# A GpSimd drain placed in the last expert of a fused linear-attention and mixture-of-experts kernel

## The chip, the core and the metric

The kernel runs on one core of a Trainium2 chip. The metric is the device time of one execution in microseconds (us); a version's time is the median of its runs. Engine names in the profile: PE is TensorE (PEld its weight loads), DVE is VectorE, ACT is ScalarE, POOL is GpSimd, SP is SyncE. A name with a q behind it (POOLq, SPq) is that engine's sequencer: semaphore waits, branches, register loads and drains run there and are not counted as busy.

## The reference

A decayed linear attention (4 batches, 8 heads, 768 steps, head dimension 64) makes 3072 token rows of 512 values, and a noisy top-2 gate sends each row to two of eight experts:

```python
state = gamma[None, :, None, None] * state + np.einsum('bhd,bhe->bhde', k[:, :, t], v[:, :, t])
y[:, :, t] = scale * np.einsum('bhd,bhde->bhe', q[:, :, t], state)
...
noisy_logits = logits + noise_scale * noise
top2 = np.argpartition(-noisy_logits, 2, axis=1)[:, :2]
...
h = np.maximum(x[mask] @ w1[e], 0.0)
out[mask] += top2_w[mask, k, None] * (h @ w2[e])
```

w1 is 512x1024 and w2 1024x512 for each expert.

## The kernel before

**The first part** (to about 100 us) does the attention in 24 chunks of 128 tokens and writes the normalized rows to `xbuf` in HBM. GpSimd has elementwise work here: `v_scale` (L302) and `q_scale` (L308), 46 instructions in all.

**The second part** handles the experts one after the other; the seven after the first are taken in an order that the counts decide. Each expert has room for 768 to 832 rows, held as blocks of 128. Row numbers per block lie in `idx`. For every block `gather` (L728) fetches rows of `xbuf` by an indirect DMA that GpSimd issues, and a DMA transpose that SP issues (L735) turns them into `xe`.

**The first layer**, `mm1` (L860 to L862), multiplies in fp16 pieces: four k-tiles of three products each (high by high, high by low, low by high), 12 matmuls per 128 hidden units, over up to half of the expert's columns. ScalarE writes the relu `hh` (L863) and VectorE the remainder `hl` (L864). There are eight such groups (`f`) in a set, and mostly two sets (`cols`) per expert. The counter `n` numbers the groups through all sets of an expert: 0 to 7 in the first, 8 to 15 in the second.

**The second layer**, `mm2` (L892 to L894), makes 24 matmuls per block of 128 rows; ScalarE scales the result into the tile `ot` (L876, four buffers), and `put` (L881) adds it to the rows of `out` by an indirect DMA with an add, again issued by GpSimd. A put waits for its `ot` from ScalarE and, since all puts add into the same tensor, for the landing of the put before it.

**Order.** The program is written under a manual schedule: each engine's queue holds its instructions in the order in which the Python code issues them. In the last expert (`e == E - 1`, room 768, six blocks) there is no next expert to gather for, so GpSimd's queue holds six puts and nothing else. With `ready = 3` the puts of blocks 0 to 2 are issued between the two sets of `mm1`, those of blocks 3 to 5 after the second set:

```python
for n0, n1 in cols:
    if n0 and ready:
        for t in range(ready):
            put(e, t, mm2(e, t))
    for f in range(FT):
        mm1(e, n0, n1, f)
```

**The end.** Behind the last put every engine reads the number of left-over blocks (L1078) and branches over the loop at L1080, which would handle rows beyond the experts' room; none are left here, so the body is not run. Then each engine waits for the outstanding DMAs and engines (semaphore waits at L1080). Leaving the tile context (L1175) ends the program: each engine runs a drain, the engines meet at a barrier led by GpSimd, GpSimd clears the semaphores, and a second barrier follows. L1171 stands for what runs ahead of the program: a drain on each engine and a few memsets on GpSimd.

Of the kernel before, what the change touches and what calls it, by code (L numbers as in the profile page):

```python
# [26 lines left out]
E, F = 8, 1024  # L27
# [70 lines left out]
def moe_kernel(ctx, tc, qT, kT, kt, vt, noise, wgn, w1, w2, ctab, qtab, xbuf, out):  # L98
    nc = tc.nc
# [83 lines left out]
    def w_load(e, which, i, n=1):  # L183

        if i == 0:
            ST[which, e] = (wpool.tile([128, 4096], F32, name="wst" + which),
                            work.tile([128, 4], F32, name="wss" + which),
                            work.tile([128, 2], F32, name="wsc" + which, bufs=3))
        src = w1 if which == "1" else w2
        src = src[ds(order[e - 1], 1)].rearrange("a p c -> (a p) c") if e else src[0]  # L190
        nc.sync.dma_start(ST[which, e][0][:, i * 1024:(i + n) * 1024], src[:, i * 1024:(i + n) * 1024])

    def w_sum(e, which, i):
        st, ss, sc = ST[which, e]
        nc.scalar.activation(junk, st[:, i * 1024:(i + 1) * 1024], AF.Square, accum_out=ss[:, i:i + 1])  # L195
        if i == 3 and e != 1:
            w_cast(e, which)

    def w_cast(e, which):
        WB[which, e] = work.tile([128, 4], BF, name="wsb" + which)  # L200
        nc.vector.tensor_copy(WB[which, e], ST[which, e][1])

    def w_scale(e, which):
        st, ss, sc = ST[which, e]
        nc.tensor.matmul(SUM[:, :4], oneb, WB[which, e], start=True, stop=True, skip_group_check=True)
        s1 = work.tile([128, 1], F32, name="s1")
        nc.vector.tensor_reduce(s1, SUM[:, :4], axis=AX.X, op=OP.add)
        pow2(s1, TW1 if which == "1" else TW2, sc[:, 0:1], sc[:, 1:2])
# [6 lines left out]
    def w_hi(e, which, i):  # L215
        st, ss, sc = ST[which, e]
        hi, lo = w_parts(which, i)
        nc.scalar.activation(hi, st[:, i * 1024:(i + 1) * 1024], AF.Copy, scale=sc[:, 0:1])  # L218

    def w_lo(e, which, i):  # L220
        st, ss, sc = ST[which, e]
        hi, lo = w_parts(which, i)
        nc.vector.scalar_tensor_tensor(lo, st[:, i * 1024:(i + 1) * 1024], sc[:, 0:1], hi,  # L223
                                       op0=OP.mult, op1=OP.subtract)
# [491 lines left out]
    def block(e, t):  # L716

        return t * 128, min(128, CAPS[e] - t * 128), NBLK * e + t

    def blocks(e):  # L720
        return range(-(-CAPS[e] // 128))

    def gather(e, t):
        o, n, i = block(e, t)
        if t == 0:
            XE[e] = XP[e % 2].tile([128, 2 * KT, CAP], F16, name="xe")
        x = XP[0].tile([128, 2 * DM], F16, name="xg", bufs=4)
        nc.gpsimd.indirect_dma_start(  # L728
            out=x[:n], out_offset=None, in_=xbuf[:128 + B0 * S] if e == 0 and t < 3 else xbuf,
            in_offset=bass.IndirectOffsetOnAxis(ap=idx[:n, i:i + 1], axis=0))  # L730
        XG[e, t] = x

    def x_t(e, t):
        o, n, i = block(e, t)
        nc.sync.dma_start_transpose(XE[e][:, :, o:o + n], XG.pop((e, t))[:n])  # L735
# [115 lines left out]
    def mm1(e, n0, n1, f):  # L851
        MM[0] += 1
        third = MM[1] and MM[0] % 3 == 0
        p = (psum2[0] if third else psum).tile([128, 512], F32, name="pH", **(dict(tag="pX") if third else dict(tag="pA", bufs=2)))
        n = n1 - n0
        for k in range(KT):
            whi = WT["1h"][:, k, f * 128:(f + 1) * 128]
            wlo = WT["1l"][:, k, f * 128:(f + 1) * 128]
            xh, xl = XE[e][:, k, n0:n1], XE[e][:, KT + k, n0:n1]
            nc.tensor.matmul(p[:, :n], whi, xh, start=(k == 0), stop=False)  # L860
            nc.tensor.matmul(p[:, :n], whi, xl, start=False, stop=False)  # L861
            nc.tensor.matmul(p[:, :n], wlo, xh, start=False, stop=(k == KT - 1))  # L862
        nc.scalar.activation(hh[:, f, n0:n1], p[:, :n], AF.Relu)  # L863
        nc.vector.scalar_tensor_tensor(hl[:, f, n0:n1], p[:, :n], 0.0, hh[:, f, n0:n1], op0=OP.max, op1=OP.subtract)  # L864

    def out_scale(e, n0, n1):
        i2 = work.tile([128, 1], F32, name="i2")
        nc.vector.tensor_tensor(i2, ST["1", e][2][:, 1:2], ST["2", e][2][:, 1:2], op=OP.mult)
        if e not in GS:
            GS[e] = work.tile([128, NBLK], F32, name="gse")  # L870
        nc.vector.tensor_scalar(GS[e][:, n0:n1], wacc[:, NBLK * e + n0:NBLK * e + n1], i2, None, op0=OP.mult)
# [7 lines left out]
    def put(e, t, ot):  # L879
        o, n, i = block(e, t)  # L880
        nc.gpsimd.indirect_dma_start(  # L881
            out=out, out_offset=bass.IndirectOffsetOnAxis(ap=idx[:n, i:i + 1], axis=0),
            in_=ot[:n], in_offset=None, compute_op=OP.add)

    def mm2(e, t, meanwhile=None):
        o, n, i = block(e, t)
        p = psum2[0].tile([128, DM], F32, name="pO", tag="pY", bufs=2)
        for f in range(FT):
            if f == 4 and meanwhile:
                meanwhile()  # L890
            a, c = hh[:, f, o:o + 128], hl[:, f, o:o + 128]
            nc.tensor.matmul(p, a, WT["2h"][:, f, :], start=(f == 0), stop=False)  # L892
            nc.tensor.matmul(p, a, WT["2l"][:, f, :], start=False, stop=False)  # L893
            nc.tensor.matmul(p, c, WT["2h"][:, f, :], start=False, stop=(f == FT - 1))  # L894
        return scaled(e, t, p)
# [122 lines left out]
    for e in range(E):  # L1018
        half = (CAPS[e] + 31) // 32 * 16
        cols = [(FIRST, 640), (640, CAPS[0])] if e == 0 else [(0, half), (half, CAPS[e])]  # L1020
        if e == 1:
            cols = [(0, 256), (256, 512), (512, CAPS[e])]
        n, more = 0, e + 1 < E

        if more:
            ahead = [lambda t=t: (gather(e + 1, t), x_t(e + 1, t)) for t in blocks(e + 1)]
        ready = 3 if not more else 0
# [3 lines that stand above are left out]
                    put(e, t, mm2(e, t))  # L1031
            for f in range(FT):
                mm1(e, n0, n1, f)
                if e:
                    if n == 2:
                        w_scale(e, "2")
                        out_scale(e, 0, NBLK)
                    if 3 <= n < 7:
                        w_hi(e, "2", n - 3)
                    if 4 <= n < 8:  # L1040
                        w_lo(e, "2", n - 4)
                    if more and n == 2:
                        w_load(e + 1, "1", 0, 2)
                        w_load(e + 1, "1", 2, 2)
                if e == 0 and n >= 7 and n < 15:
                    w_sum(1, "12"[(n - 7) // 4], (n - 7) % 4)
                if more and e and len(cols) * FT - 5 <= n < len(cols) * FT - 1:
                    w_sum(e + 1, "1", n - (len(cols) * FT - 5))
                if e == 0 and n == 14:
                    w_cast(1, "1")  # L1050
                if e == 0 and n in (1, 4, 7, 10, 13):
                    rest(1)
                n += 1
        if more and e:
            w_load(e + 1, "2", 0, 2)
            w_load(e + 1, "2", 2, 2)
            w_scale(e + 1, "1")
        todo = list(range(3, NBLK)) if e == 0 else list(blocks(e))[ready:]
        for n, t in enumerate(todo):
            if more and ahead and (e or n):  # L1060
                ahead.pop(0)()
            put(e, t, mm2_tail(e, t) if block(e, t)[1] < 128 else mm2(e, t, tables if e + n == 0 else None))
            if e == 0 and n == 0:
                w_scale(1, "1")
                w_cast(1, "2")
            if more:
                for i in ((2 * n, 2 * n + 1) if e == 0 else (n,)):
                    if i < 4:
                        w_hi(e + 1, "1", i)
                    if 1 <= i < 5:  # L1070
                        w_lo(e + 1, "1", i - 1)
                if e and 2 <= n < 6:
                    w_sum(e + 1, "2", n - 2)
            if e == 0 and n == 2:
                rank_caps()
                loop_table()
# [102 lines left out]
```

## Time and profile before

| | |
|---|---|
| median of 3 runs | 666.76 us (666.29 to 667.3) |
| the profiled execution's own time | 669.18 us |
| its span, first to last instruction | 666.9 us |
| mean granted TensorE clock | 0.99 |
| PE busy (matmuls) | 640.8 us, 96% |
| POOL busy | 201.9 us, 30%, 158 instructions |

The span is 2.28 us shorter than the profiled execution's own time, and the profiled execution is 2.42 us longer than the median of the runs. PE is at work nearly throughout; the stretch in which it is not is the end, which the 40 slices of the page show as a last digit of 1.

A row of a line's view reads: line, engine, operation and count, then shortest, median and longest duration in ns, then the starts of the first and the last one in us. A row of the timeline reads: start in us, duration in us, engine, line, operation, and in brackets how long the engine had been idle and what ended that.

### The profile page before, as it was taken

The numbers are of one execution on the slowest core, as the hardware profiler recorded it, in microseconds if no ns is written. First come the engines' busy times: TensorE is split into PE (matmuls) and PEld (weight loads), VectorE is DVE, ScalarE is ACT, GpSimd is POOL, SyncE is SP. The second block draws the span as 40 slices with busy tenths as digits, with TensorE's granted clock in tenths as the row PEclk, the third lists the DMA queues.
The fourth block names the chain that finished last, engine by engine and source line by source line (L and its number), as shares of the span: only waits on it lengthen the run. The fifth ranks groups of instructions, "written<-read, shape, count | busy, mean of one in ns | idle before, by whom it ended". The sixth has DMA issues, their size and how long they took to land.

```text
span 666.9 us, 12060 instructions
## 1 busy us (share of the span) xinstructions
PE 640.8 (96%) x4849; PEld 387.1 (58%) x4849; DVE 301.5 (45%) x723; ACT 296.3 (44%) x538; POOL 201.9 (30%) x158
## 2 busy tenths in 40 slices
PE   8999999999979999999999999999999999999991
PEld 5998887648648744554455445544554465455540
DVE  5668786799776311532153216322622262214110
ACT  5668665214525534453454344434444454433210
POOL 3555453042243034203420343034304330340111
PEclk9999999999989999999999999999999999999996
DMA  9999986967397748764675476547645782661212
GB/s 316 385 397 399 356 283 148 370 158 235 90 143 162 226 66 133 184 175 73 117 192 170 77 116 149 208 79 126 182 159 97 115 245 84 124 117 29 32 17 33
DMA packets 91001, 112.80 MB, mean 169 GB/s; under 512 B 57248, under 2 KB 57888, under 8 KB 87360
## 3 DMA queue, kind: packets, MB, share of 16 engines
q1 hardware_dynamic: 78736, 84.95, 41.5%
q0 software_dynamic: 11344, 26.22, 22.0%
q10 hardware_dynamic: 864, 0.84, 0.4%
q8 instruction: 39, 0.64, 0.4%
q14 instruction: 18, 0.15, 0.1%
HBM read 72.67 MB, written 26.21 MB: 148 GB/s over the span
## 4 chain that ended last, share of the span: by engine, by line
PE 73%; DVE 7%; DMA 3%; issue 3%; ACT 1%; POOL 1%; SPq 0%; POOLq 0%; ACTq 0%
PE pH L860 12%; PE pH L861 12%; PE pH L862 12%; PE pO L892 11%; PE pO L894 11%; PE pO L893 11%; DMA xe<-xg 2%; PE pT L906 1%; PE pT L379 1%; DVE bb L615 1%; PE pY L353 1%; DVE hl L864 1%; DMA out<-ot,idx 1%; PE pA L331 1%; DVE w2l L230 1%
## 5 line engine op out<-in xcount | busy, mean ns | idle before, releaser
L881 POOL DMA_INDIRECT out<-ot,idx x54 | 90.5, 1677 | 338.7 <-ACT ot L876 201.4
L860 PE MATMUL pH<-xe,w1h 128*128 128x384 f16 (+5 forms) x576 | 181.6, 315 | 4.3 <-DMA xe<-xg 3.6
L861 PE MATMUL pH<-xe,w1h 128*128 128x384 f16 (+5 forms) x576 | 181.6, 315 | 0.0
L862 PE MATMUL pH<-xe,w1l 128*128 128x384 f16 (+5 forms) x576 | 181.5, 315 | 0.0
L893 PE MATMUL pO<-w2l,hh 128*128 128x512 f16 x384 | 145.5, 379 | 0.4 <-DVE w2l L230 0.4
L894 PE MATMUL pO<-w2h,hl 128*128 128x512 f16 x384 | 145.5, 379 | 0.1
L892 PE MATMUL pO<-w2h,hh 128*128 128x512 f16 x384 | 145.5, 379 | 0.0
L864 DVE SCALAR_TENSOR_TENSOR hl<-pH,hh 128x384 f16<-128x384 f32 (+5 forms) x144 | 75.2, 527 | 131.1 <-ACT hh L863 129.9
L863 ACT ACTIVATE hh<-pH 128x384 f16<-128x384 f32 (+5 forms) x144 | 67.2, 468 | 135.3 <-PE pH L862 113.9
L876 ACT ACTIVATE ot<-pO,gse 128x512 f32<-128x512 f32 x48 | 33.2, 691 | 171.4 <-PE pO L894 157.6
L223 DVE SCALAR_TENSOR_TENSOR w1l<-wst,wsc,w1h 128x1024 f16<-128x1024 f32 x28 | 35.8, 1284 | 105.3 <-ACT w1h L218 105.3
L860 PEld LDWEIGHTS <-w1h 128*128 128x128 f16 x576 | 56.5, 98 | 37.0 <-issue 6.4
L728 POOL DMA_INDIRECT xg<-xbuf,idx x54 | 57.5, 1065 | 66.6 <-DVE wacc L636 31.9
L861 PEld LDWEIGHTS <-w1h 128*128 128x128 f16 x576 | 56.5, 98 | 31.5 <-issue 1.4
L862 PEld LDWEIGHTS <-w1l 128*128 128x128 f16 x576 | 56.6, 98 | 31.2
L195 ACT ACTIVATE junk<-wst 128x1024 bf16<-128x1024 f32 x64 | 67.3, 1051 | 0.0
L894 PEld LDWEIGHTS <-hl 128*128 128x128 f16 x384 | 37.6, 98 | 46.6 <-issue 1.0
L892 PEld LDWEIGHTS <-hh 128*128 128x128 f16 x384 | 37.6, 98 | 44.7 <-ACT junk L195 0.3
L893 PEld LDWEIGHTS <-hh 128*128 128x128 f16 x384 | 37.6, 98 | 44.0
L302 POOL TENSOR_TENSOR vp<-in_v,cs 128x512 f32<-128x512 f32 x24 | 26.3, 1095 | 45.6 <-issue 15.2
L218 ACT ACTIVATE w2h<-wst,wsc 128x1024 f16<-128x1024 f32 x32 | 36.6, 1142 | 1.4 <-DVE wsc L173 1.4
L218 ACT ACTIVATE w1h<-wst,wsc 128x1024 f16<-128x1024 f32 x32 | 36.2, 1141 | 1.2 <-DVE wsc L173 1.2
(168 smaller groups left out, 607.6 us busy)
## 6 DMA issues: line engine op xcount, KB each, us to landing
wst<-w SPq DMA_DIRECT2D x28, 1024.0 KB, 7.2
in_q<-qT SPq DMA_DIRECT2D x24, 256.0 KB, 5.7
in_k<-kT SPq DMA_DIRECT2D x24, 256.0 KB, 4.5
in_v<-vt SPq DMA_DIRECT2D x24, 256.0 KB, 5.5
in_kt<-kt SPq DMA_DIRECT2D x24, 256.0 KB, 6.2
xbuf<-x SPq DMA_DIRECT2D x24, 256.0 KB, 5.4
out<-zero SPq DMA_DIRECT2D x6, 1024.0 KB, 5.9
wst<-w SPq DMA_DIRECT2D x8, 512.0 KB
```

The costliest lines, as they stand in the source:

```text
L195: nc.scalar.activation(junk, st[:, i * 1024:(i + 1) * 1024], AF.Square, accum_out=ss[:, i:i + 1])
L218: nc.scalar.activation(hi, st[:, i * 1024:(i + 1) * 1024], AF.Copy, scale=sc[:, 0:1])
L728: nc.gpsimd.indirect_dma_start(out=x[:n], out_offset=None, in_=xbuf[:128 + B0 * S] if e == 0 and t < 3 else xbuf, in_offset=bass.IndirectO ...
L860: nc.tensor.matmul(p[:, :n], whi, xh, start=(k == 0), stop=False)
L861: nc.tensor.matmul(p[:, :n], whi, xl, start=False, stop=False)
L862: nc.tensor.matmul(p[:, :n], wlo, xh, start=False, stop=(k == KT - 1))
L863: nc.scalar.activation(hh[:, f, n0:n1], p[:, :n], AF.Relu)
L864: nc.vector.scalar_tensor_tensor(hl[:, f, n0:n1], p[:, :n], 0.0, hh[:, f, n0:n1], op0=OP.max, op1=OP.subtract)
L881: nc.gpsimd.indirect_dma_start(out=out, out_offset=bass.IndirectOffsetOnAxis(ap=idx[:n, i:i + 1], axis=0), in_=ot[:n], in_offset=None, com ...
L892: nc.tensor.matmul(p, a, WT["2h"][:, f, :], start=(f == 0), stop=False)
L893: nc.tensor.matmul(p, a, WT["2l"][:, f, :], start=False, stop=False)
L894: nc.tensor.matmul(p, c, WT["2h"][:, f, :], start=False, stop=(f == FT - 1))
```

## The change

Two lines are added. When the third group of the second set has been issued in the last expert (`n == 10`), a drain is issued on GpSimd's queue. It waits for no semaphore and signals none. In GpSimd's queue it stands behind the put of block 2 and ahead of the wait and the put of block 3. No other engine's instructions differ, and on GpSimd all others keep their order and their semaphores.

```diff
             for f in range(FT):
                 mm1(e, n0, n1, f)
+                if e == E - 1 and n == 10:
+                    nc.gpsimd.drain()
                 if e:
                     if n == 2:
                         w_scale(e, "2")
```

## Rows read from the trace of the kernel before

**Rows 1.** The page: the span in 40 slices (PE, POOL) and the chain that ended last.
```profile
span 666.9 us, 12060 instructions
...
PE   8999999999979999999999999999999999999991
...
POOL 3555453042243034203420343034304330340111
...
PE 73%; DVE 7%; DMA 3%; issue 3%; ACT 1%; POOL 1%; SPq 0%; POOLq 0%; ACTq 0%
```

**Rows 2.** Timeline of GpSimd in the last expert: the six puts.
```profile
612.22 1.56 POOL L881 DMA_INDIRECT out<-ot,idx  x1 [13.49 <-ACT ot L876]
619.16 1.56 POOL L881 DMA_INDIRECT out<-ot,idx  x1 [5.38 <-DMA out<-ot,idx]
624.65 1.56 POOL L881 DMA_INDIRECT out<-ot,idx  x1 [3.94 <-ACT hh L863]
643.40 1.56 POOL L881 DMA_INDIRECT out<-ot,idx  x1 [17.19 <-ACT ot L876]
648.95 1.56 POOL L881 DMA_INDIRECT out<-ot,idx  x1 [3.99 <-ACT ot L876]
654.35 1.56 POOL L881 DMA_INDIRECT out<-ot,idx  x1 [3.84 <-DMA out<-ot,idx]
```

**Rows 3.** Line 1175, the end of the program: drains and barrier waits by engine.
```profile
L1175 POOLq EVENT_SEMAPHORE  x4: 17/17/17, 666.2 to 666.8; - x4
L1175 SPq DRAIN  x3: 7/7/13, 659.9 to 666.4; - x3
L1175 POOLq DRAIN  x3: 51/103/5616, 660.5 to 666.7; - x3
L1175 ACTq DRAIN  x2: 8/8/8, 660.1 to 666.4; - x2
L1175 DVEq DRAIN  x2: 10/14/17, 660.3 to 666.4; - x2
L1175 PEldq DRAIN  x2: 8/8/8, 660.6 to 666.4; - x2
```

**Rows 4.** Line 1175 again, in the window 656 to 666.2 us alone.
```profile
L1175 POOLq DRAIN  x1: 5616/5616/5616, 660.5 to 660.5; - x1
```

**Rows 5.** Busy time by engine in four windows of the end, then granted clock, DMA share, GB/s.
```profile
655.90:658.80 2.90, 0.00 (x0) 0.00 (x0) 0.00 (x0) 0.00 (x0) 0.01 (x1) 0.64 0.69 90
658.80:660.40 1.60, 0.00 (x0) 0.00 (x0) 0.00 (x0) 0.00 (x0) 0.00 (x0) 0.50 0.02 5
660.50:666.10 5.60, 0.00 (x0) 0.00 (x0) 0.00 (x0) 0.00 (x0) 0.00 (x0) 0.50 0.00 0
666.10:666.90 0.80, 0.00 (x0) 0.00 (x0) 0.00 (x0) 0.00 (x0) 0.00 (x0) 0.50 0.00 0
```

**Rows 6.** What SP's queue waited for from 650 us: total, times, longest, in us.
```profile
SPq L1175 <- PEq L1175: 6.8, 2, 6.3
```

**Rows 7.** Line 1171, the start of the program: GpSimd's drain there, and its last memset.
```profile
L1171 POOLq DRAIN  x1: 188/188/188, 0.3 to 0.3; - x1
...
L1171 POOL MEMSET const-uint8-127<- x1: 116/116/116, 0.3 to 0.3; 128x1 uint8 x1
```

**Rows 8.** GpSimd's groups over the whole span: count, then busy us, mean ns.
```profile
L881 POOL DMA_INDIRECT out<-ot,idx x54 | 90.5, 1677 | 338.7 <-ACT ot L876 201.4 <-DMA out<-ot,idx 69.4 <-ACT junk L195 31.7
L728 POOL DMA_INDIRECT xg<-xbuf,idx x54 | 57.5, 1065 | 66.6 <-DVE wacc L636 31.9 <-issue 15.1 <-DVE idx L643 12.0
L308 POOL TENSOR_TENSOR qs<-in_q,gq 128x512 f32<-128x512 f32 x22 | 28.1, 1278 | 2.9 <-DMA in_q<-qT 1.5 <-DVE am L334 1.4
L302 POOL TENSOR_TENSOR vp<-in_v,cs 128x512 f32<-128x512 f32 x24 | 26.3, 1095 | 45.6 <-issue 15.2 <-PE pU L362 13.0 <-DMA in_v<-vt 9.0
```

**Rows 9.** Line 881 in the windows 626 to 644 us, and 643 to 667 us.
```profile
L881 POOLq EVENT_SEMAPHORE  x2: 17/2542/5067, 629.5 to 643.2; - x2
...
DMA to landing us min/median/max: 4.6/4.6/4.6
```

**Rows 10.** Timeline of ScalarE: the three last tiles `ot`.
```profile
642.44 0.69 ACT L876 ACTIVATE ot<-pO,gse 128x512 f32<-128x512 f32 x1 [4.74 <-PE pO L894]
647.62 0.69 ACT L876 ACTIVATE ot<-pO,gse 128x512 f32<-128x512 f32 x1 [4.49 <-PE pO L894]
652.80 0.69 ACT L876 ACTIVATE ot<-pO,gse 128x512 f32<-128x512 f32 x1 [4.49 <-PEq L1080]
```

**Rows 11.** Line 1080 in the window 654 to 667 us: the waits for all outstanding work.
```profile
L1080 POOLq EVENT_SEMAPHORE  x13: 17/43/2345, 654.9 to 660.3; - x13
```

**Rows 12.** Timeline of GpSimd at 144 us: the first put, right behind gathers.
```profile
144.55 1.17 POOL L728 DMA_INDIRECT xg<-xbuf,idx  x1 [0.30 <-issue]
146.02 2.86 POOL L881 DMA_INDIRECT out<-ot,idx  x1 [0.30 <-issue]
```

## The prediction
> **What bounds the kernel now.** I read the page first. Its slices show PE at nine tenths or more almost everywhere, and the chain that ended last is 73% PE [rows 1]. GpSimd is busy 30% of the span, so an instruction more on it looks free at first sight. The one slice that is not PE's is the last, so I went there with the timeline of GpSimd and the views of the two lines that end the program.
>
> In the last expert GpSimd issues six puts. The first three start at 612.22, 619.16 and 624.65 us, then GpSimd stands idle for 17.19 us until the fourth at 643.40 us; the last starts at 654.35 us and takes 1.56 us [rows 2]. Its data has landed 4.6 us after its start [rows 9], at about 658.9 us; in the window from 655.90 to 658.80 us DMA still moves 90 GB/s, afterwards next to nothing [rows 5]. The waits for all outstanding work are passed by 660.3 us [rows 11]. By then there is nothing left to do, and yet the span goes on to 666.9 us.
>
> The rows of line 1175 say why. Each engine runs a drain there. On SP, ACT, DVE and PE one takes 7 to 17 ns. On GpSimd there are three, of 51, 103 and 5616 ns [rows 3], and the long one is the first, at 660.5 us [rows 4]. It ends at 660.5 + 5.6 = 666.1 us. In exactly this window no engine is busy and no DMA moves a byte [rows 5]. The other engines stand at the barrier behind it: SP for 6.3 us [rows 6] (the view puts that down to PE's sequencer, whose drain at 660.6 us was over in 8 ns, so it was GpSimd's). After the long drain 0.8 us are left. So **5.62 us, 0.84% of the span, are one drain of GpSimd, all of it on the path that sets the end.** This is what an added drain has to do with.
>
> **The change part by part.** Nothing is removed or moved; one drain is added, behind put 2 and ahead of the wait for put 2's landing and put 3.
>
> *The added drain.* It can begin when put 2 is through on GpSimd, at 624.65 + 1.56 = 626.21 us [rows 2]. No row shows a drain at this place. The bounds are the shortest and the longest GpSimd drain, 0.05 us and 5.62 us [rows 3]. I take the long end, since like the long one it is the first behind many indirect DMAs. Then it ends at 631.8 us. Queued behind it are a semaphore wait, which put 2's landing opened at 629.5 us and which passes at once when reached later, and put 3, which is held until its `ot` is ready: the queue's next wait begins only at 643.2 us [rows 9], and `ot` is made from 642.44 to 643.13 us [rows 10]. The drain has 643.13 - 626.21 = 16.9 us and needs at most 5.6. Cost on the path: 0, hidden by the second set of first-layer products and the second layer of block 3 on PE. Were that cover gone, every microsecond would count in full: puts 3, 4 and 5 start 5.55 and 5.40 us apart, while their tiles are ready every 5.18 us [rows 2, 10], so the puts are held by each other's landings, and a late put 3 makes the end late by as much.
>
> *The drain at the end.* Whether the time moves at all is decided by what its 5.62 us depend on. Three observations speak for work that piles up between drains. It was the first drain since the one at the start: that one took 0.19 us, beside a memset of 0.12 us [rows 7], and the two behind the long one, with no instruction of work in between, took 0.10 and 0.05 us [rows 3]. Nothing else was in progress for it to wait for [rows 5]. And GpSimd had issued 54 puts and 54 gathers since the start [rows 8]: 5616 / 108 = 52 ns for each. With the added drain 105 of these 108 are settled in the middle, and three are left for the end: 3 x 52 = 0.16 us, a value between the drains of 0.05 and 0.19 us that found little to do. Gain: 5.62 - 0.16 = 5.46 us. The bounds are 5.57 us (only 0.05 us left) and 0 (all of it stays); I take 5.46, near the former, because the rows with little before them are all under 0.2 us.
>
> The other engines do not limit this: the last of them, PE, is at the barrier at 660.6 us [rows 3], and GpSimd would be there at 660.5 + 0.16 = 660.7 us.
>
> *Sum.* In the profiled execution 669.18 + 0 - 5.46 = 663.72 us; it stood 2.42 us above the median, which I keep as it is: 666.76 - 5.46 = **661.30 us**. The likeliest case's own range is 660.7 us (the fastest run, 666.29, less 5.57) to 662.0 us (the slowest run, 667.3, less 5.3).
>
> **The rivals.**
>
> *A fixed price: no change.* The long drain may cost the same after any indirect DMA, however many, as if it asked all queues once. Three puts still come between the added drain and the end, so the end would again pay 5.62 us, and the added one is hidden: 666.76 us. For it: no row shows a second drain behind indirect DMAs, and 52 ns for each is a quotient, not a row. Against it: nothing moves during the drain [rows 5]. To the same time leads that the added drain does not reach GpSimd's cores at all and only passes its sequencer, as the 7 to 17 ns of the other engines do [rows 3].
>
> The Trainium skill (PSUM — Partial Sum Buffer, section Engine vs sequencer instructions) says that a drain waits for the engine to go fully idle. By that rule a drain keeps no account of old work, the same three puts stand ahead of the end as before, and the time would stay at 666.76 us. The trace bears the rule out only in part: GpSimd's last busy row ends at 655.91 us, 4.6 us before the long drain begins, so no row shows what that drain waits for. I give the fixed price with all its ways 28%.
>
> *Half and half.* If part is fixed and part piles up, or only the latest few DMAs are on account, the gain lies between: half of 5.46 us gives 664.0 us. For it speaks only that it can't be excluded: 7%.
>
> *Slower: the added drain outlasts its cover.* If a drain amid running engines and DMAs is much dearer than one at rest, put 3 is late and the end with it, microsecond by microsecond. The place is GpSimd's queue ahead of put 3; the mechanism decides from 16.9 us on, three times the long drain. With no gain at the end, a drain of 22.5 us (four times the long one) would give 666.76 + 22.5 - 16.9 = 672.4 us. Waiting also for put 2's landing at 629.5 us would only make it end at 635.1 us. A smaller price at the same place: a put that finds GpSimd in another state took 2.86 instead of 1.56 us [rows 12], 1.3 us. 5%.
>
> **How the numbers follow.** Work that piles up has 60%, half and half 7%, the fixed price 28%, slower 5%. About 0.2%, 1.3 us, is what a measurement of this kernel can tell from no change. Faster by more than that: 60 + 7 = 67%. Within it: 28%. Slower: 5%. The predicted time is that of the likeliest, 661.3 us. As the likeliest holds only 60%, the range must take in the fixed price: 660.7 to 667.3 us, the upper end being the slowest run of before. It leaves out the slower case and the tails of the others.
>
> **What would show it.** In the profile after, line 1035 has a GpSimd drain that starts at about 626.2 us, takes some 5.5 us and ends far ahead of 643 us; the puts 3 to 5 keep their distances; line 1175 has three GpSimd drains all under 0.3 us, and the span ends about 0.9 us after 660.5. With the fixed price, both the new drain and the first at line 1175 take 5.6 us. If the new one takes 0.1 us and the last 5.6, the added drain does not do what the last one does. I am wrong in the cover if the idle time ahead of put 3 grows over 17.2 us.

## The result, and the profile after

| | before | after |
|---|---|---|
| median | 666.77 us (6 runs, 666.29 to 667.3) | 661.2 us (6 runs, 660.16 to 662.26) |
| ratio, 95% interval | | 0.9902 (0.9882 to 0.9921) |
| span of the profiled execution | 666.9 us | 658.1 us |
| added drain | none | 9.34 us |
| first GpSimd drain of the program's end | 5.62 us | 0.30 us |

The kernel is faster by 5.6 us in the medians. The quotient of the two medians is 0.9916 and lies inside the interval of the measured ratio, 0.9902. The lines that answer to [rows 3], line 1177 of the changed kernel (engine and operation, count, shortest/median/longest in ns, first and last start in us):

```profile
L1177 POOLq EVENT_SEMAPHORE  x4: 17/17/17, 657.3 to 658.0; - x4
L1177 SPq DRAIN  x3: 7/7/13, 656.6 to 657.5; - x3
L1177 POOLq DRAIN  x3: 51/103/297, 656.9 to 657.8; - x3
L1177 PEldq DRAIN  x2: 8/8/8, 657.3 to 657.6; - x2
```

The two short drains are what they were, and the long one has gone from 5616 to 297 ns. SP, which stood at the barrier for 6.3 us [rows 6], now stands there for 0.8 us:

```profile
SPq L1177 <- PEq L1177: 1.3, 2, 0.8
```

The added drain, line 1035 of the changed kernel:

```profile
L1035 POOLq DRAIN  x1: 9342/9342/9342, 621.1 to 621.1; - x1
```

And GpSimd's timeline in the last expert, which answers to [rows 2]:

```profile
615.81 1.56 POOL L881 DMA_INDIRECT out<-ot,idx  x1 [5.52 <-DMA out<-ot,idx]
621.28 1.56 POOL L881 DMA_INDIRECT out<-ot,idx  x1 [3.91 <-ACT hh L863]
639.91 1.56 POOL L881 DMA_INDIRECT out<-ot,idx  x1 [17.07 <-ACT ot L876]
645.53 1.56 POOL L881 DMA_INDIRECT out<-ot,idx  x1 [4.06 <-ACT ot L876]
650.99 1.56 POOL L881 DMA_INDIRECT out<-ot,idx  x1 [3.90 <-DMA out<-ot,idx]
```

The drain's row opens at 621.1 us, before put 2 itself runs, and closes at 630.4 us, 7.6 us after put 2 is through (621.28 + 1.56 = 622.84 us). Put 3 still starts 9.5 us later, at 639.91 us, and the idle time ahead of it has not grown: 17.07 us against 17.19.

The spans differ by 8.8 us, more than the medians. From the start of put 5 to the end it was 666.9 - 654.35 = 12.6 us and is now 658.1 - 650.99 = 7.1 us: 5.4 us of the difference arise here. The other 3.4 us lie ahead of the added drain, where no instruction differs: put 2 started at 624.65 us and now at 621.28. Most of them (2.95 us by the last rows shown) arise near 190 us, at the gathers for the second expert. Before:

```profile
186.45 1.62 POOL L881 DMA_INDIRECT out<-ot,idx  x1 [0.31 <-issue]
193.56 0.99 POOL L728 DMA_INDIRECT xg<-xbuf,idx  x1 [5.50 <-DMA xe<-xg]
198.02 1.59 POOL L881 DMA_INDIRECT out<-ot,idx  x1 [3.46 <-DMA out<-ot,idx]
```

After:

```profile
186.81 1.62 POOL L881 DMA_INDIRECT out<-ot,idx  x1 [0.30 <-issue]
191.82 1.00 POOL L728 DMA_INDIRECT xg<-xbuf,idx  x1 [3.40 <-DMA xe<-xg]
195.07 1.59 POOL L881 DMA_INDIRECT out<-ot,idx  x1 [2.25 <-DMA out<-ot,idx]
```

I take that for a difference between executions, not of the change: the profiled execution of before was 2.4 us above its median, that of after (660.38 us) 0.8 us below its own. A kernel of the experiments below ("Behind the last put") shows the size of it: its instructions are those of before up to and with put 5, and its put 5 starts 4.07 us earlier than the 654.35 us of before:

```profile
650.28 1.56 POOL L881 DMA_INDIRECT out<-ot,idx  x1 [3.88 <-DMA out<-ot,idx]
```

So of two traces only the stretch behind the edit is compared here. In that stretch hardly anything but the drain differs: from the start of put 5 to the end of the span, less the first GpSimd drain of the program's end, it is 6.9 us before and 6.8 us after, and 6.4 to 6.9 us in every experiment that has no added drain behind put 5.

### The profile page after: what moved, and what is told of

The parts are those of the page before. It is cut to its first block, busy times and chain, and to the rows that moved or that the text cites. A ratio compares the mean times of both kernels' runs of the same rounds, so it can differ in the third digit from the quotient of the medians.

```text
span 658.1 us, 12061 instructions
## 1 busy us (share of the span) xinstructions
PE 640.0 (97%) x4849; PEld 386.6 (59%) x4849; DVE 301.9 (46%) x723; ACT 295.7 (45%) x538; POOL 201.5 (31%) x158
## 4 chain that ended last, share of the span: by engine, by line
PE 75%; DVE 9%; ACT 1%; issue 1%; DMA 1%; POOL 0%; POOLq 0%; ACTq 0%
PE pH L860 12%; PE pH L861 12%; PE pH L862 12%; PE pO L892 11%; PE pO L893 11%; PE pO L894 11%; PE pT L906 1%; PE pT L379 1%; DVE bb L615 1%; PE pY L353 1%; DVE hl L864 1%; DMA out<-ot,idx 1%; PE pA L331 1%; DVE a L607 1%; ACT junk L195 1%
```

## The experiments

All are the kernel before with small edits. "On account" means those of the indirect DMAs issued by GpSimd since its last drain that the next drain has still to settle; at first it is taken to be all of them.

### What the long drain depends on

**Ahead of all indirect DMAs.** The drain is queued in the first part, ahead of the first gather.

```diff
+    at(19, nc.gpsimd.drain)
     for t in range(3):
         at(19 + (t > 0), gather, 0, t)
```

> The drain is moved to the first part, ahead of the first indirect DMA, behind some 40 elementwise operations. Piling up by DMA: a drain takes 0.145 us + 0.0507 us per indirect DMA since GpSimd's last drain (from 5616 ns with 108 and 297 ns with 3); the added one takes under 0.3 us, the one at the end 5.6 us, time unchanged at 666.8 us. A price paid once by the first drain behind work: 5.6 us here, 0.3 us at the end, time 661.3 us. Piling up by elementwise operations: some 5 us here, under 1 us at the end.

Measured: one run of 664.86 us; one run cannot tell 2 us, so the drains decide. The added one:

```profile
L837 POOLq DRAIN  x1: 2617/2617/2617, 93.1 to 93.1; - x1
```

GpSimd's timeline around it:

```profile
93.05 1.30 POOL L302 TENSOR_TENSOR vp<-in_v,cs 128x512 f32<-128x512 f32 x1 [2.54 <-issue]
94.31 1.29 POOL L308 TENSOR_TENSOR qs<-in_q,gq 128x512 f32<-128x512 f32 x1
```

The drain waits for the two operations ahead of it (to 94.31 + 1.29 = 95.60 us) and ends at 93.1 + 2.6 = 95.7 us. At the end of the program nothing has changed:

```profile
L1176 POOLq DRAIN  x3: 45/103/5611, 656.2 to 662.3; - x3
```

So it is neither a price that the first drain pays once, nor the elementwise operations. The long drain needs indirect DMAs ahead of it.

**With 45 left for the end.** The drain stands in the fifth expert's first set, 63 indirect DMAs behind the start.

```diff
                 mm1(e, n0, n1, f)
+                if e == 4 and n == 2:
+                    nc.gpsimd.drain()
```

> The drain is moved to the idle stretch of the fifth expert: 63 indirect DMAs stand ahead of it, 45 between it and the end. Piling up: the drain at the end takes 0.145 + 45 x 0.0507 = 2.43 us, the time is 666.8 - 3.2 = 663.6 us. Paid once: 0.3 us at the end, 661.3 us. Fixed price: 5.6 us at the end, 666.8 us. The added drain by piling up takes 0.145 + 63 x 0.0507 = 3.3 us, times 1.4 if work on other engines stretches it as it did in the changed kernel.

Measured at the end:

```profile
L1177 POOLq DRAIN  x3: 51/103/3728, 655.1 to 659.3; - x3
```

3.73 us lies between all and nothing: the fixed price is out. It is also more than the 2.43 us of a line through 108 and 3 DMAs. Each DMA costs more than the 52 ns of the prediction, and 108 of them cost less than 108 times as much. (The single run took 661.87 us.)

**Timed again.** The same kernel in more rounds.

> The drain in the fifth expert once more, now timed. Its drain at the end took 3.73 us (45 DMAs on account), 1.89 us less than before: ratio 0.9972, time 1.9 us under the kernel before, and 3.4 us above the changed kernel.

Median 663.17 us beside 665.32 us of before in the same session, ratio 0.9977 (0.9957 to 0.9996); the drain at the end was again of 3728 ns, and 0.9972 was expected. That agrees with the shorter drain, though the interval, a gain of 0.3 to 2.9 us, is wide.

**With 5 and 6 left, and VectorE idle or busy.** Two kernels put the drain right behind put 0, and ahead of it.

```diff
                 for t in range(ready):
                     put(e, t, mm2(e, t))
+                    if t == 0:
+                        nc.gpsimd.drain()
```

> The drain stands behind the put of block 0, where VectorE is idle for 15 us while PE works and the put is in flight. The added drain of the changed kernel took 7.55 us once put 2 was through, by piling up 5.47 were expected. If VectorE's instructions stretch it: 0.145 + 103 x 0.0507 = 5.4 us here once put 0 is through. If the put in flight or PE's work stretches it: 7.5 us. The drain at the end, 5 DMAs: 0.4 us. Time as the changed kernel, 661.3 us.

```diff
                 mm1(e, n0, n1, f)
+                if e == E - 1 and n == 2:
+                    nc.gpsimd.drain()
```

> The drain stands ahead of the put of block 0, in the first set of first-layer products, where VectorE is busy over nine tenths of the time. If VectorE's instructions stretch it: more than 10 us, lasting until VectorE falls idle, with put 0 a little late. If it is the put in flight: 7 us, as in the changed kernel. The drain at the end, 6 DMAs: 0.45 us. Time as the changed kernel or up to 1 us more.

Behind put 0 (VectorE idle), the added drain and the end:

```profile
L1033 POOLq DRAIN  x1: 10209/10209/10209, 607.6 to 607.6; - x1
...
L1177 POOLq DRAIN  x3: 51/103/460, 655.9 to 656.9; - x3
```

Ahead of put 0 (VectorE busy):

```profile
L1035 POOLq DRAIN  x1: 10242/10242/10242, 593.4 to 593.4; - x1
...
L1177 POOLq DRAIN  x3: 51/103/542, 656.8 to 657.9; - x3
```

VectorE makes no difference: both take 10.2 us, and 8.4 us from the moment that the put ahead is through. VectorE was busy for 0.00 us of the 8.4 in the first kernel and for 5.96 in the second (not the nine tenths that I had expected). If VectorE stretched the drain, I had expected 5.4 us in the first and over 10 us in the second; as both take the same, that theory falls. If it was the put in flight, I had expected 7.5 and 7 us; that came nearer, without being met. The drain behind put 0 also made put 1 late (idle ahead of it 9.19 us in place of 5.38), which the idle stretch ahead of put 3 took up. The drains at the end, 0.46 and 0.54 us for 5 and 6 DMAs, lie on one line with 0.30 us for 3 and 3.73 us for 45: **0.05 us and 0.082 us for each.** Single runs were of 659.42 and 660.50 us.

### Whether the cover is needed

**Between puts 4 and 5.**

```diff
             put(e, t, ...)
+            if e == E - 1 and t == 4:
+                nc.gpsimd.drain()
```

> The drain stands between the puts of blocks 4 and 5, where it has no cover: put 5 is due 3.8 us after put 4 is through. Five drains so far fit 0.05 us + 0.082 us for each indirect DMA on account. 107 DMAs on account give 8.8 us, put 5 starts 5.2 us late, and the time is 666.8 - 5.5 + 5.2 = 666.5 us. If the account holds some 77 by then (68 is what the 5616 ns of the kernel before amount to, with 108 issued), 6.3 us, put 5 2.7 us late, 664.0 us. If the drain were harmless here, 661.3 us.

GpSimd's last puts:

```profile
646.89 1.56 POOL L881 DMA_INDIRECT out<-ot,idx  x1 [4.00 <-ACT ot L876]
656.77 1.56 POOL L881 DMA_INDIRECT out<-ot,idx  x1 [8.32 <-issue]
```

And the drain at the end:

```profile
L1177 POOLq DRAIN  x3: 51/103/133, 662.5 to 663.4; - x3
```

Put 5 starts 9.88 us after put 4 in place of 5.40 [rows 2], 4.48 us late; the drain at the end is 5.48 us shorter. (I had expected 5.2 or 2.7 us.) That leaves 1.0 us, ratio 0.9985; measured was 0.9988 (0.9964 to 1.0011), no change that can be told. Without cover the drain costs nearly what it saves.

**Behind the last put.**

```diff
             put(e, t, ...)
+            if e == E - 1 and t == 5:
+                nc.gpsimd.drain()
```

> The drain stands right behind the last put, where only the landing of that put (4.6 us) covers it. With 68 DMAs on account it runs from 655.9 to 661.5 us by the clock of the kernel before; the register load, the branch and the waits that had run in its stead follow, some 2.4 us, and the drain at the end takes 0.05 us: 664.5 us. If a drain waits for the landing first: about 666.8 us as before.

Ratio 1.0003 (0.9988 to 1.0018), 665.27 us beside 665.42: nothing gained, as the second of the two cases named. The drain:

```profile
L1064 POOLq DRAIN  x1: 9291/9291/9291, 650.1 to 650.1; - x1
```

It ends at 659.4 us, 7.5 us after put 5 is through at 650.28 + 1.56 = 651.84 us, although the same DMAs on account took 5.6 us at rest. The put's landing, 4.6 us after its start, is at 654.9 us. A drain with a put in flight does not do all its work during the flight.

**In every expert.** Seven drains.

```diff
                 mm1(e, n0, n1, f)
+                if e and n == (10 if e == E - 1 else 2):
+                    nc.gpsimd.drain()
```

> One drain in the idle stretch of every expert but the first, the last of them where the changed kernel has it: 21, 14, 14, 14, 14, 13, 15 DMAs on account, and 3 at the end. By 0.05 + 0.082 us per DMA, counted from when the put ahead of it is through: 1.8, 1.2, 1.2, 1.2, 1.2, 1.1, 1.3 us, and 0.30 us at the end; all covered, time as the changed kernel, 661.2 us. A fixed price per drain would show equal durations.

```profile
L1035 POOLq DRAIN  x7: 4382/6388/8160, 205.1 to 619.4; - x7
```

```profile
L1177 POOLq DRAIN  x3: 51/103/292, 655.6 to 656.5; - x3
```

The time is as expected, 659.43 us beside 665.42, ratio 0.9908 (0.989 to 0.9926); the durations are not. Three of the seven by themselves, with 14, 14 and 15 DMAs on account:

```profile
L1035 POOLq DRAIN  x1: 8160/8160/8160, 271.0 to 271.0; - x1
...
L1035 POOLq DRAIN  x1: 4382/4382/4382, 339.3 to 339.3; - x1
...
L1035 POOLq DRAIN  x1: 5557/5557/5557, 619.4 to 619.4; - x1
```

The puts ahead of them and their landings, from the same kernel:

```profile
271.23 1.45 POOL L881 DMA_INDIRECT out<-ot,idx  x1 [3.73 <-DMA out<-ot,idx]
...
DMA to landing us min/median/max: 7.3/7.3/7.3
...
339.50 1.39 POOL L881 DMA_INDIRECT out<-ot,idx  x1 [3.28 <-DMA out<-ot,idx]
...
DMA to landing us min/median/max: 3.5/3.5/3.5
...
619.64 1.56 POOL L881 DMA_INDIRECT out<-ot,idx  x1 [4.09 <-ACT hh L863]
...
DMA to landing us min/median/max: 4.7/4.7/4.7
```

They land at 278.5, 343.0 and 624.3 us; the drains end at 279.2, 343.7 and 625.0 us, each 0.6 to 0.7 us later; of two more whose landing the trace gives, one ends 0.6 us and one, with 21 on account, 0.9 us later. So **a drain here also waits until the last indirect DMA has landed.** This is what made the added drains longer than expected. The stretches of the first two shown were not idle: a gather stood behind each drain and started 0.8 us after its end, at 279.94 and 344.43 us. The drain held it up, but the time does not show it.

**With nothing in flight.** The drain where the changed kernel has it, behind a memset of one column of put 2's tile, which has to wait for that put's landing. The column is written again before it is used.

```diff
-                    put(e, t, mm2(e, t))
+                    ot = mm2(e, t)
+                    put(e, t, ot)
+                    if t == 2:
+                        nc.gpsimd.memset(ot[:, :1], 0.0)
+                        nc.gpsimd.drain()
```

> The drain stands where the changed kernel has it, but behind a memset of one column that waits until put 2 has landed, so that it begins with no DMA in flight while PE, ScalarE and VectorE work. If a drain amid work first waits for the landing of the last put and the account is the 65 that the drain at the end suggests, it takes 5.4 us from its start. If 105 are on account, 8.6 us. If other engines' work stretches it, 7.5 us, as it took in the changed kernel once put 2 was through.

```profile
623.81 0.10 POOL L1034 MEMSET ot<- 128x1 f32 x1 [3.14 <-DMA out<-ot,idx]
...
L1035 POOLq DRAIN  x1: 5510/5510/5510, 623.8 to 623.8; - x1
```

5.51 us, while PE was busy for all of them, VectorE for 1.7 us and ScalarE for 1.1 us: as at rest with 65 on account (5.36 us) and the memset of 0.1 us. Other engines' work did not stretch this drain, and 105 issued DMAs are 65 on account. (The single run took 659.37 us.)

### How many are on account

**More DMAs.** A gather of 16 rows is added ahead of each gather, into a tile that nothing reads.

```diff
+        xd = work.tile([128, 2 * DM], F16, name="xd", bufs=1)
+        nc.gpsimd.indirect_dma_start(out=xd[:16], out_offset=None, in_=xbuf[:128 + B0 * S] if e == 0 and t < 3 else xbuf,
+                                     in_offset=bass.IndirectOffsetOnAxis(ap=idx[:16, i:i + 1], axis=0))
         XG[e, t] = x
```

> The kernel before with one more indirect gather of 16 rows ahead of every gather, into a tile that nobody reads: 162 indirect DMAs in place of 108; it is slower by the added waits, and only the drain at the end matters. If the account takes every DMA alike without a limit: 0.05 + 162 x 0.082 = 13.3 us. If it is limited to some 68 to 100 DMAs: 5.6 to 8.2 us. If it counts rows rather than DMAs, little more than 5.6 us.

```profile
L1178 POOLq DRAIN  x3: 51/103/3574, 670.8 to 674.9; - x3
```

None of the expected values: 162 DMAs end in a shorter drain than 108, (3574 - 52) / 81.7 = 43 on account. The account does not only grow. (The run took 677.51 us, the added waits among it.)

**87 left for the end.** The drain in the second expert.

```diff
                 mm1(e, n0, n1, f)
+                if e == 1 and n == 2:
+                    nc.gpsimd.drain()
```

> The drain is moved to the second expert: 21 indirect DMAs ahead of it, 87 between it and the end. By 0.05 + 0.082 us per DMA the drain at the end takes 7.2 us, 1.5 us more than without any added drain, and the kernel is 1.5 us slower than before, ratio 1.0023. If the account is limited to 68 DMAs: 5.6 us, no change.

```profile
L1177 POOLq DRAIN  x3: 51/103/4053, 657.0 to 661.6; - x3
```

4.05 us, 49 on account in place of 87, and the kernel is faster, not slower: 663.28 us beside 665.32, ratio 0.9959 (0.9943 to 0.9976). The drain alone gives 1.56 us, 0.9977, a hair outside; what the rest is stays open.

**59, 73 and 98 left.** These three were run because the size of the account, a term of the prediction's sum, was still open: between 45 and 87 it had to be cut by some 40.

```diff
                 mm1(e, n0, n1, f)
+                if e == 3 and n == 2:
+                    nc.gpsimd.drain()
```

with `e == 2` for 73 and `e == 0` for 98.

> The drain is moved to the fourth expert: 59 indirect DMAs between it and the end. Drain at the end by 0.05 + 0.082 us per DMA on account: 4.9 us if the account is not cut before 59, 1.6 us if it has been cut by 40. A limit that only caps it (at 49, or 68) would give 4.1 or 4.9 us.

> The drain is moved to the third expert: 73 indirect DMAs between it and the end. Drain at the end: 6.0 us if not cut yet, which is longer than the 5.6 us of the kernel before although fewer DMAs stand ahead of it; 2.8 us if cut by some 40.

> The drain is moved to the first expert: 98 indirect DMAs between it and the end. One cut of 38 to 40: 58 to 60 on account, a drain of 4.8 to 5.0 us at the end. A second cut: 18 to 22 on account, 1.5 to 1.9 us.

The drains at the end with 59 left:

```profile
L1177 POOLq DRAIN  x3: 51/103/4870, 658.9 to 664.3; - x3
```

With 73 left:

```profile
L1177 POOLq DRAIN  x3: 51/103/6013, 659.4 to 665.9; - x3
```

With 98 left:

```profile
L1177 POOLq DRAIN  x3: 51/103/4829, 657.9 to 663.3; - x3
```

All three at a value that was named for the cut: 59 and 73 count in full, 98 count as 58.5. Together:

| issued since the last drain | 1 | 3 | 5 | 6 | 45 | 59 | 73 | 87 | 98 | 108 |
|---|---|---|---|---|---|---|---|---|---|---|
| drain at the end, ns | 133 | 297 | 460 | 542 | 3728 | 4870 | 6013 | 4053 | 4829 | 5616 |
| on account, (ns - 52) / 81.7 | 1.0 | 3.0 | 5.0 | 6.0 | 45.0 | 59.0 | 73.0 | 49.0 | 58.5 | 68.1 |

Somewhere between 73 and 87 the account loses some 38 to 40, and then grows on. So an early drain can make the end worse: with 73 left it takes 6.01 us, 0.4 us more than with no added drain at all. Up to 73 it counts DMAs and not rows: the 14 from 45 to 59 and the 14 from 59 to 73 cost 81.6 ns each, although four of these 28 move only 32 or 48 rows, and those of 128 rows in the last expert cost 81.7. The single runs were of 666.90, 668.47 and 665.84 us.

### The changed kernel once more

> The changed kernel once more, timed in more rounds. The drains alone account for 5.62 - 0.30 = 5.32 us, a ratio of 0.992 to the kernel before. A ratio below 0.990 would need a second source of gain.

Median 660.35 us (658.91 to 662.57) beside 665.32, ratio 0.9926 (0.9900 to 0.9952); the drains were of 9107 and 297 ns. The 0.992 of the drains lies inside this interval and, at its edge, inside that of the first measurement, so a second source of gain is not needed; these intervals, some 0.4 to 0.5% wide, would not show one of a microsecond. No version tried beats the changed kernel: the one with a drain in every expert has the same ratio within the intervals.

## Where the prediction was right, and which step failed

- **What bounds the end: right.** The idle drain of 5.62 us was on the path. With it cut, SP stands at the barrier for 0.8 us in place of 6.3.
- **"Work that piles up between drains": right in kind.** A drain ahead of all indirect DMAs changed nothing at the end; 45 of them left 3.73 us. The fixed price, at 28%, falls with that. So does the reading of the Trainium skill's rule (PSUM — Partial Sum Buffer, section Engine vs sequencer instructions: a drain waits for the engine to go fully idle) as one that keeps no account. What the rule says is seen ahead of all indirect DMAs, where the drain ended 0.1 us after the last operation ahead of it. The wait for the landing and the account, both after GpSimd's last busy row, go beyond it.
- **"5616 / 108 = 52 ns for each": the mis-sized term.** A DMA on account costs 82 ns and the drain itself 0.05 us; the quotient came out low because only 68 of the 108 were still on account. For three DMAs this gives 0.30 us in place of 0.16, and a gain of 5.62 - 0.30 = 5.32 us in place of 5.46. As only three DMAs were left, the error is 0.14 us. With more left it would have been large: at 52 ns each, 73 DMAs take 3.8 us, where 6.01 us were measured.
- **The added drain, "5.62 us": wrong in size, without effect.** Its row is of 9.34 us, 7.6 of them behind put 2. That it waits for the landing I had named only as an aside to the slower rival. The cover held: the bound was 16.9 us.
- **The cover: right.** Between puts 4 and 5 the drain made put 5 4.48 us late, and most of the gain was gone.
- **The time: the middle right, the lower edge of the range the step that failed.** The median came out at 661.2 us against a forecast of 661.3; to agree within 0.1 us, where the six runs lie 2.1 us apart, is luck. And the measured ratio gives 0.9902 x 666.77 = 660.2 us (658.9 to 661.5), 0.5 us below the stated 660.7. That edge was "the fastest run, 666.29, less 5.57": it took the spread of three runs, 1 us, as the whole spread of a comparison. The runs showed more: those of the kernel before lay between 664.31 and 670.06 us in one later session, two measurements of the changed kernel differ by 0.0024 (1.6 us) in their ratios, and two kernels with the same instructions up to put 5 reached it 4.07 us apart. The mis-sized term above does not explain the low time; it works the other way. By the drains the ratio is 0.9920, 661.4 us, inside the stated range and inside the measured interval; the 1.2 us between that and 660.2 are put down to spread because hardly anything but the drain differs at the end, and no run shows them one by one.

## What to carry to other kernels

Read the sequencers' rows at the very end of a program, not only the engines' busy time: this kernel, with 108 indirect DMAs from GpSimd, paid for them once more in GpSimd's last drain, where nothing covered it. An extra drain late in the kernel, in a stretch in which GpSimd is idle for longer than a landing and the whole account, took that work off the end here; the closer to the end the better, as long as the cover lasts. Before taking a price from one row and a count, vary the count: the quotient of a single point hid both the true price and the cut.

## What the runs showed that I had not expected

- The account is cut by some 38 to 40 DMAs somewhere between 73 and 87 issued. Why there stays open. The 162 DMAs that ended at 43 have lost 119, three times some 40: a cut each time that the account comes near 80 would give that, and one cut at 108 and at 98. That is a reading of one run; 54 of its DMAs moved 16 rows, and DMAs of different sizes were not tried one by one.
- The semaphore operation INC_SWDGE_SEM at the end counts the same account. Before, in line 1080:

```profile
L1080 POOLq INC_SWDGE_SEM  x1: 1552/1552/1552, 654.9 to 654.9; - x1
```

  After, in line 1082:

```profile
L1082 POOLq INC_SWDGE_SEM  x1: 253/253/253, 651.6 to 651.6; - x1
```

  With 45 on account it took 1098 ns: from 3 and 45 follow 0.19 us and 20 ns for each, which gives 68 for the 1552 ns of before, the number that its drain gives too. With 73 and 87 left it took 1657 and 1178 ns, by the same line 73 and 49, so it shows the cut as well. It lies beside the landing of the last put, so its 1.3 us are no gain.
- With a put in flight and 14 or 15 DMAs on account a drain ended 0.6 us after the landing; behind the last put, with 68, it ended 4.5 us after it, and in the two kernels with the drain beside put 0, with some 62, 4.2 and 4.3 us after it. That is 0.5 to 1.1 us less than the same account takes at rest; the drain in the fifth expert, with 63, ended 3.4 us after it, 1.8 us less. So part of the work is done before the landing; which part, and what decides it, is not settled.
